# A tuned attention-plus-Fourier-plus-MLP kernel: the first part's steps taken in another written-out order, with other PSUM banks

## The chip, the cores and the metric

The kernel runs on one core of a Trainium2 chip. The metric is the device time of one execution, in microseconds (us). Engines are named as in the profile: PE is TensorE's products, PEld its weight loads, DVE is VectorE, ACT is ScalarE, POOL is GpSimd, SP is SyncE, which starts the DMAs. L766 is line 766 of the kernel. PSUM, which takes TensorE's products, is used as eight banks, numbered 0 to 7.

## The reference

Attention with positive random features, then a layer in the manner of FNet. Input are q, k and v of shape (8, 8, 576, 64), omega (128, 64), and two weight matrices, 512 x 2048 and 2048 x 512.

```
def phi(x):                                   # x: q or k times 64**-0.25
    h = x @ omega.T - sum(x * x) / 2          # 128 features
    return exp(h - max(h)) / sqrt(128)
kv  = k_p.T @ v ;  z = sum(k_p)               # for each of the 64 heads
num = q_p @ kv  ;  den = q_p @ z + 1e-6
x   = (num / den), heads side by side         # (8, 576, 512)
u   = x + real(fft(fft(x, axis=1), axis=2))
un  = layernorm(u)
out = u + relu(un @ w_ch1) @ w_ch2
```

## The kernel before, in words

The kernel has two parts, each one call of `Listing.run` (L283): part one at L1704, until about 418 us of the profiled execution, and part two at L2440. Part two does the MLP of 4096 of the 4608 rows, in a scheme that replaces eight block products by seven; its lists of the order are not touched and it is left out here.

**What part one computes.** The 64 heads are taken two at a time: 32 head pairs, four to a batch. For pair n, `attn` (L697) issues these steps:

- *Transposes of k and q*, "T": nine 128 x 128 tiles in three groups, of 4, 4 and 1 (`transposed`, the product at L636). Each group takes a bank, and ScalarE or VectorE copies it to SBUF (`evicted`, L640).
- *Scores*, "P": k and q times omega, in three groups of 4, 1 and 4 tiles (`pairs_of`, L716, the products at L731). In form Q these are products of 64 x 64 tiles, four for a tile of scores (16, 4 and 16 products), in form R of 64 x 128 tiles (8, 2 and 8); the profile counts twice as many. Each group takes two banks next to each other (a "duo"). Behind it stands the softmax: VectorE finds the maxima (L673), ScalarE takes the exponentials (L690), which also empties the banks.
- *The kv step*, "kv" (L766): 36 products in 64 x 64 tiles for one head pair, each of which the profile counts as two (x72), into a duo; `keep` (L775) copies the result out.
- *Transposes of q's features*, "E": groups of 1, 4 and 4 tiles, again at L636.
- *The nd step*, "nd" (L814 and L822): 20 products in 128 x 64 tiles, x36 in the profile, with numerator and denominator together. VectorE (or ScalarE) divides (L831 to L843), which writes x.

As soon as the four pairs of a batch are there, `mix(b)` (L855) does its Fourier transform: folds on VectorE and GpSimd (L863), two first-stage steps on TensorE (L933 and L947, here "F"), three second-stage steps (L993 and L1004, "C"), then the sum with x (`residual`, L1034) and the store of u.

Beside these run: the loads of k, q, v and the tables; the weights' conversion from the 64-bit input on ScalarE, VectorE and GpSimd (`narrow`, L548, by `weights`, L578); the MLP of the first 512 rows in the plain way, four blocks of 128 rows (`plain_of`, L1260: 16 hidden steps at L1293, "h", evicted at L1275 or L1277, and output steps at L1318, "o", which end in the addition at L1332 in `rest`, L1327); and what part two wants ready: transposed rows (`ahead`, L1633), sums of tokens (`block_norms`, L1442), of w2's parts (`w2_parts`, L1525) and of w1's parts (`weight_sums`, L1615, four sums on VectorE at L1622).

**What sets the order.** Every one of these pieces of work is a Python generator that yields a `Step` (which engines can do it, which banks and buffers it takes and gives back, which events it waits for) ahead of the instructions of that step. The head pairs are three such streams (`pairs`, L1629), of pairs 0, 3, 6, ..., of 1, 4, 7, ... and of 2, 5, 8, ...; there are thirteen streams at the start, and a stream can fork others off. `Listing.run` takes one step at a time from those that wait, and the order in which the steps are taken is the program order on each of the engines. [...]

Three written-out lists fix what it takes, for part one:

- PICKS (L68): one character a step. Its value, divided by 36, tells the engine (0 or 1, where a step can go on two), and the rest the number of the waiting stream that goes next:

```
return [divmod(DIGITS.index(c), 36) for c in text]
```

- BANKS (L91): one digit for each step that takes a bank or a duo: the bank, or the first of the two.

```
i = int(self.given[self.taken])
return i, max(t, *self.banks[i : i + n])
```

- FORMS (L101): one word for each TensorE step, read by `form()` (L421): W the whole 128 x 128 array, C 128 x 64 halves, Q 64 x 64 quarters, R 64 x 128 halves by row; two or three letters for the Fourier steps, which have several kinds of products.

The costs in the `Step`s are a planner's; where a list gives the pick they only decide nothing more than whether a step's events and buffers are there at all. A step may be taken only once everything it waits for has been taken before it; semaphores between the engines are put in from the data that the instructions read and write.

Of the kernel before, what the change touches and what calls it, by code (L numbers as in the profile page):

```python
# [41 lines left out]
class Clock(NamedTuple):  # L42
# [23 lines left out]


PICKS = (  # L68
    "1g30geg03ghid3dddehciMfegcdgej8ijgRNd8dih3gifjhbhf8hKhebgcgcijhebkl9fdcbmbN0kidhakjjdOb7f79i9baeSdja"
    "jbbScifhjgbTgfibgdijdjhjfijfabibbjdcjdiaShjhdSfdjcbfbfjjgbb9ffcgkkekhjkQecgSiki8chifjhefadfcggQgQc9d"  # L70
    "babadgcdakOb8fha8e9gfhfgg8ff1ffdPfbecffffce9e7c7fehhhbhhhhjhb8giejTijLjj7ig978ijijecdTjih8ejgfgbQgfk"
    "f88efhkkVfllWh9k9Tb8McmallmN8jkkklllkc7lmjnhfhhmoopVjcen8eaihjSbcjdekggmjbbnlohRI9linmb89eMeggWmdlhi"
    "mkeklOkfgjgURdgjbhdldkldelgmWgehkchjgifidhbbihec9fkicjbalihhbj60ijj6L96ijji7adi7edR8kjl7k6mdceeclnPe"
    "9jpfkh3Xjin95a7mekaal8bihhklmn4jgmfj7jnH8ooeeiebeko8cg9jkbifponpkpLnkkppRccSgegmmklcldX6bebdnhhWchie"
    "dSgkcmnmG7hclLaallfkjfdjnimSiiaV9ecd8kfkcT8ejjbbh6ghfd48aggghgahgcfiPghggb6gcddgg5bdhfdeiija5LjTidcc"
    "759g9gSahNce7hefigUlggck9cljafjgelagXicL8khailaRkilgiajbgeQhb7djjgihicjkahc8dbclMkhggjjcbkjjabjkkicc"
    "d7ljlaecd7ki9c5akkVbdllkaa67Klcjl9ighi6jfj77kkjIdmm9nlmlcm9loebhbno8QinZngkf#gqnpjmjkrlmj6jqknlg9llj"
    "jicjciiolii7hcQ6cafh7hgcgk59eiibibbii7Selllcl8jjml9c58ncf7dlelfFfdnm97k7l8di5lhlmm7j7lhlmen6jiLP8lgn"
    "nnnXggmmmfnoj9okfhlop8hnpllgjgIkknn9Xhhngonen9YlhjYWlhoY7hppqhr4ahlmkhffqqkqoroeqaenkdngp9ZZ955el99j"
    "ggih5kagf9n7gnd5cqcpdhfm9m9mlaXoaiJmkm8gmgnigfnnngga5akellaVacmmkVVm74cmg5mml9hgii7lllhppm9rmpptokpo"  # L80
    "qjjmqlqIo7qdlplZmoq76qqbXooknhclijlOkhgghjgf5gemijgfPiVhjUdllkhglikigLlgkGejdiPddbjkmheenganil50WWWW"
    "ma4lhfKbj5I77fJ9Mc90bebeeef4aHeadfc5aecb5fL89hObffadfgdchhcadgfhiibKS9kbgkLhgcQa9dIcbdb77gie79I8aiJU"
    "kK3hdJ9g9469Pd6baf8efe6idiajcHTT8kdbkdiien6mNpZpPpblOeOo5hePcSkLb32aHfhiSSeeaab76eiLai3ffgbfj7difmj8"
    "68dhcfil3dgl6n7nnXmWddQickli69fdiNOgaNgc9cEdI7abehijd9kkfah5Sia5aa7e9de595cad8ac24dbccb5dNbbaae6cffc"
    "hi7LO6bJbdaaddeaPb6dacgb8bfdN9b8KdfecccFgLfPRbQSi6Rc7ijhjk31O%%%%%%tjttb12f5s1J7q8aqqq89ppF5peqj4Yde"
    "enmgoXXnXgm4njQ1lj0NmLbeo33bf0dm81Un1ehAlggl60jkkQ6jjjjkjlikl9jlmiTc9ngnla08mfncgm8ogmjmccfjabib59fe"
    "hleb7j3j49djj7g7hL7h6g6QaidiIc360ff075efg5794h7a5ged7dgEhh8ffff43a094896b9b72b2baE322267360636645544"
    "43300100"
)

BANKS = (  # L91
    "3012406207460426047614204702610424206742764064210461702606425016437042604670426420340276450214620462"
    "0154240623024602432023602476105246103240736247021640524026704672047501647240264320620340260462460262"
    "4052361420652430517205647602642064605427135703462040267450231462402456406521346062023460201026026064"
    "3172260467420642301602450647201320460345627402467064246042673402646207143672167204231602465421240643"
    "7426462740516207246121046042654723450173602660512046721451706257067312"
)

FORMS = (  # L101
# [6 lines left out]
)  # L108


# [2365 lines left out]
```

## Time and profile before

| | before |
|---|---|
| median of 3 runs | 1112.19 us (1110.9 to 1112.87) |
| profiled execution | 1113.75 us |
| its span | 1112.0 us |
| granted TensorE clock in it | 1.000 |
| instructions of PE, PEld, DVE, ACT, POOL | 17759, 17759, 1685, 1644, 404 |

Part one by itself (0 to 418 us) and part two, as the view by stretches of time gives them:

```profile
0.00:418.00 418.00, 402.73 (x7850) 335.04 (x7851) 342.36 (x763) 299.47 (x1051) 185.84 (x210) 1.00 0.66 200
418.00:1112.00 694.00, 688.75 (x9911) 588.88 (x9909) 539.99 (x922) 239.18 (x593) 204.01 (x194) 1.00 0.71 221
```

In such a row stand the stretch, its length, the busy time and number of instructions of PE, PEld, DVE, ACT and POOL, the granted clock as a share of full speed, the mean busy share of the 16 DMA engines, and GB/s. In a row of the timeline stand the start in us, the length in us, the engine, the line, the operation, "out<-in" by the program's names, sizes and types, the number of instructions in the row, and in brackets the idle time before it with what ended it. In the list of waits a row names the waiting engine and line, what released it, the total in us, how often, and the longest. "issue" is idle time that nothing in the profile ended.

### The profile page before, as it was taken

The numbers are of one execution on the slowest core, as the hardware profiler recorded it, in microseconds if no ns is written. First come the engines' busy times: TensorE is split into PE (matmuls) and PEld (weight loads), VectorE is DVE, ScalarE is ACT, GpSimd is POOL, SyncE is SP. The second block draws the span as 40 slices with busy tenths as digits, with TensorE's granted clock in tenths as the row PEclk, the third lists the DMA queues.
The fourth block names the chain that finished last, engine by engine and source line by source line (L and its number), as shares of the span: only waits on it lengthen the run. The fifth ranks groups of instructions, "written<-read, shape, count | busy, mean of one in ns | idle before, by whom it ended". The sixth has DMA issues, their size and how long they took to land.

```text
span 1112.0 us, 42246 instructions
## 1 busy us (share of the span) xinstructions
PE 1091.5 (98%) x17759; PEld 923.9 (83%) x17759; DVE 882.4 (79%) x1685; ACT 538.7 (48%) x1644; POOL 389.9 (35%) x404
## 2 busy tenths in 40 slices
PE   8899999999999999999999999999999999999998
PEld 7788888878878676799998668998667999667998
DVE  6899999996776766688697777898667898668895
ACT  6988888865725554624214453223563223341221
POOL 2343444524655537733613455000365000152000
PEclk9999999999999999999999999999999999999999
DMA  7856756566665568798798768757678756556553
GB/s 230 222 177 194 242 177 202 173 191 179 222 224 211 186 183 314 228 294 299 246 300 297 215 201 254 215 158 238 203 213 259 226 156 216 174 157 220 152 160 112
DMA packets 196590, 236.80 MB, mean 213 GB/s; under 512 B 53808, under 2 KB 120624, under 8 KB 196400
## 3 DMA queue, kind: packets, MB, share of 16 engines
q1 hardware_dynamic: 195904, 233.83, 68.3%
q8 instruction: 140, 2.29, 0.9%
q14 instruction: 50, 0.41, 0.1%
q10 hardware_dynamic: 496, 0.26, 0.1%
HBM read 182.13 MB, written 56.10 MB: 214 GB/s over the span
## 4 chain that ended last, share of the span: by engine, by line
PE 92%; ACT 3%; DVE 3%; issue 1%; DMA 1%; POOL 0%; SPq 0%; DVEq 0%; ACTq 0%; POOLq 0%
PE banks L2259 30%; PE banks L1806 27%; PE banks L731 5%; PE banks L1293 5%; PE banks L1318 5%; PE banks L636 5%; PE banks L1958 4%; PE banks L766 3%; PE banks L814 2%; ACT e L690 2%; PE banks L933 2%; PE banks L993 2%; PE banks L947 1%; DVE nmx L673 1%; PE banks L822 1%
## 5 line engine op out<-in xcount | busy, mean ns | idle before, releaser
L2259 PE MATMUL banks<-wl,sums 128*64 128x128 f32 x3584 | 217.2, 273 | 0.1
L2259 PEld LDWEIGHTS banks<-wl,sums 128*64 128x64 f32 x3584 | 201.0, 137 | 2.4 <-issue 0.5
L690 ACT ACTIVATE e<-banks,nmx 128x128 f32<-128x128 f32 x576 | 161.3, 425 | 24.3 <-DVE nmx L673 23.9
L673 DVE TENSOR_REDUCE nmx<-banks 128x8 f32<-128x1024 f32 (+1 forms) x96 | 89.3, 953 | 25.6 <-PE banks L731 21.3
L2259 PE MATMUL banks<-wl,hid 128*64 128x128 f32 x1536 | 98.4, 273 | 0.5 <-DVE part L2234 0.5
L2259 PEld LDWEIGHTS banks<-wl,hid 128*64 128x64 f32 x1536 | 87.6, 137 | 1.7 <-DVE part L2234 0.7
L1806 PE MATMUL banks<-unw,wxw 128*64 128x256 f32 x704 | 85.8, 379 | 0.0
L2229 ACT ACTIVATE s<-banks 128x128 f32<-128x128 f32 x112 | 30.9, 277 | 109.7 <-PE banks L2259 109.7
L731 PE MATMUL banks<-om,kqT 64*64 64x128 f32 (+1 forms) x1988 | 81.7, 278 | 1.2 <-ACT e L690 0.8
L731 PEld LDWEIGHTS banks<-om,kqT 64*64 64x64 f32 (+1 forms) x1988 | 67.4, 143 | 12.8 <-issue 4.7
L2259 PE MATMUL banks<-wl,hx 128*64 128x128 f32 x1152 | 73.4, 273 | 0.4 <-DVE part L2234 0.4
L1806 PE MATMUL banks<-rx,wxw 128*64 128x256 f32 x576 | 71.2, 379 | 0.0
L1806 PEld LDWEIGHTS banks<-unw,wxw 128*64 128x64 f32 x704 | 50.6, 137 | 24.7
L1806 PE MATMUL banks<-ttw,wxw 128*64 128x256 f32 x576 | 70.2, 379 | 0.0
L1831 ACT ACTIVATE s<-banks 128x512 f32<-128x512 f32 x65 | 38.5, 596 | 64.2 <-PE banks L1806 59.2
L576 POOL TENSOR_TENSOR w<-w,raw 128x512 f32<-128x512 f32 x28 | 38.3, 1372 | 86.3 <-DVE raw L570 86.3
L2259 PEld LDWEIGHTS banks<-wl,hx 128*64 128x64 f32 x1152 | 65.3, 137 | 1.2 <-DVE part L2234 0.6
L1293 PE MATMUL banks<-unT,w 128*64 128x128 f32 (+1 forms) x744 | 64.5, 276 | 0.0
L2308 POOL TENSOR_TENSOR more<-more,part 128x512 f32<-128x512 f32 x2 | 2.7, 1340 | 172.6 <-ACT part L2301 172.6
L1293 PEld LDWEIGHTS banks<-unT,w 128*64 128x64 f32 (+1 forms) x744 | 58.9, 158 | 2.5 <-issue 1.2
L1318 PE MATMUL banks<-w,ht 128*128 128x512 f32 (+1 forms) x152 | 59.0, 597 | 0.0
L1806 PEld LDWEIGHTS banks<-rx,wxw 128*64 128x64 f32 x576 | 41.4, 137 | 20.2
(289 smaller groups left out, 2387.6 us busy)
## 6 DMA issues: line engine op xcount, KB each, us to landing
wl<-w2l SPq DMA_DIRECT2D x245, 256.0 KB, 3.9
wxw<-w1x SPq DMA_DIRECT2D x120, 256.0 KB, 3.2
raw<-in_moe_w_ch_dram SPq DMA_DIRECT2D x32, 512.0 KB, 4.7
kq<-in_k_dram SPq DMA_DIRECT2D x32, 288.0 KB, 4.2
kq<-in_q_dram SPq DMA_DIRECT2D x32, 288.0 KB, 4.6
vd<-in_v_dram SPq DMA_DIRECT2D x32, 288.0 KB, 5.0
ur<-us SPq DMA_DIRECT2D x30, 256.0 KB, 4.9
w2l<-sums SPq DMA_DIRECT2D x14, 512.0 KB, 3.9
```

Source lines behind the costliest of these rows:

```text
L576: eng.tensor_tensor(out=dst, in0=dst, in1=lof, op=ALU.add)
L636: nc.tensor.transpose(ps[:, (j - j0) * 128 : (j - j0 + 1) * 128], src(j), ident[:])
L673: nc.vector.tensor_reduce(nmx[:, :, 0:num], pps[:, :, 0 : MF * num].rearrange("p b (c m) -> p b c m", m=MF), axis=AX.X, op=ALU.max, negate ...
L690: nc.scalar.activation(out=e[:, c + (i if num == 1 else 0), :], in_=pps[:, i, MF * c : MF * c + MF], func=AF.Exp, bias=nmx[:, i, c : c + 1],)
L731: nc.tensor.matmul(pps[cols, c, MF * m : MF * m + MF], lhsT=kqT[rows, j, cols], rhs=om2[rows, :],)
L766: nc.tensor.matmul(kvp[cols, i, 0 : D + 1], lhsT=feature(r)[rows, cols], rhs=vds[n % NV][rows, r, :], start=(r == 0), stop=(r == R - 1),)
L1293: nc.tensor.matmul(hp[cols, 0:TP], lhsT=w1[:, dc, 128 * fc : 128 * fc + 128][:, cols], rhs=unTs[key][:, dc, :], start=(dc == 0), stop=(dc ...
L1318: nc.tensor.matmul(yp[cols, 0:DM], lhsT=hs[fc][:, 128 * i : 128 * i + 128][:, cols], rhs=w2[:, fc, :], start=(fc == 0), stop=(fc == NFC - ...
L1806: nc.tensor.matmul(ps[half, span * f : span * f + span].rearrange("f (b q) -> f b q", q=Q), lhsT=left[:, P * f : P * f + P][:, half], rhs= ...
L1831: nc.scalar.activation(out=s[:], in_=ps, func=AF.Copy)
L1958: nc.tensor.matmul(cell[half].rearrange("f t (b q) -> f t b q", q=Q), lhsT=w[:, d, col : col + 128][:, half], rhs=right[:, :, d].rearrange ...
L2259: nc.tensor.matmul(ps[half, 0:128], lhsT=left[:, f][:, half], rhs=wls[head(j), i, n][:, f], start=start and f == 0, stop=(f == 3), skip_gr ...
```

## The change

Three strings are replaced: PICKS, BANKS and FORMS of part one. Nothing else is edited. Read out with the kernel's own generators, both orders have the same 1908 steps (498 on TensorE, 463 on ScalarE, 489 on VectorE, 133 on GpSimd, 213 on SP, the others on no engine), each on the same engine and in the same form; FORMS changes only because the steps that read it come in another order. 365 of the bank digits differ. The order of SP's steps is the same.

```
 PICKS = (
-    "1g30geg03ghid3dddehciMfegcdgej8ijgRNd8dih3gifjhbhf8hKhebgcgcijhebkl9fdcbmbN0kidhakjjdOb7f79i9baeSdja"
...
+    "1g0fgf5gf04f1dhcQbe3dgdf0d6h8ShQgdibhkb6fblhfhegLjidadegigjbibgideb7fc8Rhiic8jf8fiiejablTjkjfghjfkcl"
...
 BANKS = (
-    "3012406207460426047614204702610424206742764064210461702606425016437042604670426420340276450214620462"
...
+    "0624046724650423140762062346276041602456074246020467234620642365723046204230426420340267420361420462"
...
 FORMS = (
-    "4W 2Q W R 3W 4Q 6W Q W C R 2W 2Q 3W 3Q C 3W R 2W C W 3Q 2W Q 4W 4Q C Q 7W 3Q C W WQ 3W WQ W R 2Ccz Q W 2R C 5W Q "
...
+    "4W 2Q 2W R W Q W 2Q 3W Q 3W C R Q 2W Q W Q 3W Q W Q C Q 3W R 2W C 2Q W 2Q 5W 4Q C Q 7W 3Q C W WQ 3W WQ W R 2Ccz "
...
```

What the strings mean can't be read from them. Decoded, TensorE's order around six places reads as follows (the times are those of the profile before; the number is the head pair; P8 and P32 are score groups of one and of four tiles in form Q, P16 one of four tiles in form R, by their counts of products in the profile):

| about | before | after |
|---|---|---|
| 49 us | P32(5) nd3 kv5 E5 T6 | P32(5) nd3 kv5 T6 E4 |
| 79 us | kv7 E7 E7 E7 C0 nd6 nd7 | kv7 E7 T8 T8 E6 E7 E7 C0 nd6 nd7 |
| 132 us | P kv11 P32(13) E11 h nd12 kv13 | P32(13) kv11 h E11 nd12 kv13 |
| 266 us | kv25 h kv23 E23 h E25 | kv25 P8(23) P32(23) h E25 h E24 E25 kv23 E23 E23 h E23 E25 |
| 296 us | P32(28) P8 kv26 P32(28) C C h h h | P32 P8 P32(28) kv26 h C C h h h |
| 356 us | P16(31) P16(29) kv29 kv31 E31 | P16(29) P16(31) kv31 kv29 E29 |

More of the change, by code (lines that the diff above doesn't have):

```diff
@@ L68 @@
 PICKS = (
[L69 to L88, printed above, removed]
+    "1g0fgf5gf04f1dhcQbe3dgdf0d6h8ShQgdibhkb6fblhfhegLjidadegigjbibgideb7fc8Rhiic8jf8fiiejablTjkjfghjfkcl"
@@ new lines @@
+    "heghk9lPgRhhidjiejLdkeldild9fi7fjfgkjejjjhhidcefje8gddiOge8hidlfPail7baibffbdhP7fjdjbeKebiiaTjiSaghb"
+    "dhcdca7fekPebiheeiefgahhfgfih8O1eaggegffhddhhhac977K8aiighih8hii7Sdhdj7jfjfajdiiePdgheeacifSe9efiekg"
+    "9hkkhlikUl9lVfTajRbic8iijjk8kkhkjdkMgjh9eelhoeSlciioib7n8giggon9jnffjkfjadmbaINooogaafkmeemlooUmknkl"
+    "WLagXmnmhhiemakRlgkkhkklhdfkgmhgojgWbdmJPgbfjeimljhigefbnghc6a0legfbi7e7jh67hhggbkkf7lm8kcfcelVlemmK"
+    "k6d9mnmmcklbd3gVcle8eka5k7blliellllm79jjjdnojHokolkihbaWljfmlk4jlgillaUaeimkKgnbmninebnblbbcTGkifgWf"
@@ new lines @@
+    "lfSjmagldlkklililjgbkgfeXm6hTfeghdjdTbekJ9kh8i8hf7deif4aggagghhg6eihi7jjj8Qhhfcggf79cggeedeg8ab5bf5i"
+    "gPdgeaSiSi8Pgihlk9kbieeknkelmLokkhPhfcibjagl7NdllkkeidO9i8h9jiSgiki5ch9gahRdijhfjhdi9jcjjbcbfj6hhidi"
+    "cbbfd96k88fd9ji9i978g8eMibg76kfkdigbclmk8jf9K7flhWamamccnk7jk6ki9qmoHpeZ7fg9Xnoihdnnnodlnhhpgkhnk6kg"
+    "lk8ieaajj5df6kkggdjdjjOh77idiGgcif78Riakf9lkkkk5hljjjjfeikk6mhmjecWgj7eigmfba5g78lneh6lnXbjn8nnnnclg"
+    "mmkkWbnl6lmlmfhnnkjlpihpkk9H8hhnfkhjnmmg9leVll9YljklbViojZiqgkgqrjhXmnhlkg63niawwawvadcucv+qv7axq6c6"
@@ new lines @@
+    "pu963vw8k64uqSivjvlttttoktttvophripqiruut5ouYrn&4deuhrmrjt3hqsiittluu$tvwr#weMuvefneomqqfuvusoouurrv"
+    "melejqul(poqpututslo&sssuvrwovpqSvZqqpsZtsomqnUndpsuhjmQlkjos%rj$kspmrlrqsnornqpdoilslr#rsg1pT0#ghZp"
+    "sm!k$ltgSQgpbkPbfhknhlmhbkkkiimempehgrTghiimOhnnoopgigpkkgkpgokjYkqppjURkoiQYopZZmgbjljjjfpjqljogonj"
+    "nTTjmnQYlnnhWeighXSgocmjjqoqkellQ#ppsVhpfulVjt(vntjdlkpmrVbqgn!aqchObegOWmhfUpZZbYrijrrjdpphhttMtouf"
+    "riuuosmfVslrfstYt&rptrojcvVe%ckrtgihfrqrpTfgnrqpijmdfjqpppoXkpdkmfijihfennahlcgddkgmhUjmekfopnRhmXjj"
@@ L89 @@
+    "nkhmqUYpkeeQijhnklliekhXlkllnhhhmpimmlnpN!!hkY#rpVrsbiihrphmU$ht#h%%%%%tpkttb1ssrqr1soor$sq#Ns#fqPnl"
+    "gdeNoTbhggekl0lMaOgo0a0d8Ka9dllVm0k66dkllglikj0Raiiigjhkkjdcm8O0j9l9lbflmnol8jh3nndkhg9kk8j9heh8jafe"
+    "cag3J9k9k3ba9bbifhI2Pa8fc7390dd39g50cb8a472fb5a2c8fg5afa3Chhf7g5ggg2h2g8cd9eGb7572735725077712726643"
+    "13220100"
 )
 BANKS = (
-    "3012406207460426047614204702610424206742764064210461702606425016437042604670426420340276450214620462"
-    "0154240623024602432023602476105246103240736247021640524026704672047501647240264320620340260462460262"
@@ L94 @@
-    "4052361420652430517205647602642064605427135703462040267450231462402456406521346062023460201026026064"
-    "3172260467420642301602450647201320460345627402467064246042673402646207143672167204231602465421240643"
-    "7426462740516207246121046042654723450173602660512046721451706257067312"
+    "0624046724650423140762062346276041602456074246020467234620642365723046204230426420340267420361420462"
+    "0140206405625462704670620341526250345643021624016402360462506524603210436024602167045274604602064621"
@@ L97 @@
+    "4025013426052346271462102602426402043672563075264020564250160740620465264015406260240162046706204762"
+    "0643062446026406251040624013426702406342150620456232042642304062464650175241732046025467517704260234"
+    "2650642352647346560246170426234670126374264204256071406702347046413702"
 )
 FORMS = (
[6 rows of a table removed]
[6 rows of a table added]
 )
```

12 rows, old and new, of the table FORMS are left out of this document.

## The prediction

> **What bounds the kernel now.** The page comes first: which engine is full, at what clock, and what the chain of waits is made of.
>
> ```profile
> span 1112.0 us, 42246 instructions
> PE 1091.5 (98%) x17759; PEld 923.9 (83%) x17759; DVE 882.4 (79%) x1685; ACT 538.7 (48%) x1644; POOL 389.9 (35%) x404
> ...
> PEclk9999999999999999999999999999999999999999
> ...
> q8 instruction: 140, 2.29, 0.9%
> ...
> PE 92%; ACT 3%; DVE 3%; issue 1%; DMA 1%; POOL 0%; SPq 0%; DVEq 0%; ACTq 0%; POOLq 0%
> ```
>
> TensorE is busy 98% of the span at full clock and carries 92% of the chain. An order alone can win only from the rest: 3% ScalarE, 3% VectorE, 1% "issue". Part one ends near 418 us; by stretches of 25 us it reads so (busy us of PE, PEld, DVE, ACT, POOL; clock; DMA):
>
> ```profile
> 50.00:75.00 25.00, 23.94 (x515) 20.54 (x513) 23.93 (x59) 22.53 (x85) 7.73 (x8) 1.00 0.39 128
> ...
> 100.00:125.00 25.00, 24.49 (x562) 21.79 (x561) 23.79 (x60) 20.06 (x69) 12.50 (x13) 1.00 0.81 246
> ...
> 200.00:225.00 25.00, 25.00 (x545) 21.07 (x538) 23.92 (x45) 21.82 (x81) 12.81 (x14) 1.00 0.54 164
> ...
> 250.00:275.00 25.00, 23.57 (x574) 20.80 (x574) 14.34 (x29) 14.66 (x56) 10.46 (x10) 1.00 0.58 173
> ...
> 350.00:375.00 25.00, 23.80 (x403) 18.57 (x400) 18.45 (x52) 14.89 (x54) 10.08 (x15) 1.00 0.55 189
> ```
>
> Up to about 225 us VectorE (23.8 to 23.9 of 25) and ScalarE (20 to 22.5) are nearly as full as TensorE: a microsecond saved on TensorE there is partly lost to the next wait for an eviction. After 225 us both fall to 14 to 18 of 25, and TensorE alone sets the pace: what it saves there is saved in full.
>
> Third view: TensorE's waits from 20 to 400 us (total, times, longest).
>
> ```profile
> PE banks L766 <- issue: 2.1, 3, 1.2
> PE banks L814 <- issue: 1.7, 2, 1.3
> PE banks L636 <- ACT e L690: 1.5, 4, 0.6
> PE banks L636 <- issue: 1.4, 1, 1.4
> PE banks L993 <- issue: 1.0, 1, 1.0
> PE banks L731 <- ACT e L690: 0.8, 2, 0.6
> PE banks L636 <- DVE x L843: 0.6, 2, 0.3
> PE banks L822 <- issue: 0.5, 1, 0.5
> ```
>
> The larger share, 2.1 + 1.7 + 1.4 + 1.0 + 0.5 = 6.7 us in eight idle times, is "issue": no semaphore ended it. The timeline of TensorE shows the three of over 1 us after 225 us, and the one before:
>
> ```profile
> 49.26 0.74 PE L814 MATMUL banks<-kv,qeT 128*64 128x65 f32 x18 [1.29 <-issue]
> ...
> 264.90 1.06 PE L1293 MATMUL banks<-unT,w 128*128 128x128 f32 x8
> 265.79 0.27 PE L636 MATMUL banks<-ident,e 128*128 128x128 f32 x1
> 267.50 1.91 PE L636 MATMUL banks<-ident,e 128*128 128x128 f32 x16 [1.43 <-issue]
> ...
> 296.47 0.27 PE L993 MATMUL banks<-sd_sb,y 128*64 128x128 f32 x1 [1.02 <-issue]
> ...
> 356.89 0.34 PE L766 MATMUL banks<-vd,e 64*64 64x65 f32 x6 [1.20 <-issue]
> ```
>
> They strike in the middle of a step, after a run of kv (line 766) and nd (814, 822) steps. The count of instructions between the ends of such stalls tells why:
>
> ```profile
> 49.26:79.41 30.15, 28.65 (x634) 24.92 (x634) 27.72 (x68) 27.26 (x101) 8.87 (x10) 1.00 0.48 153
> ...
> 267.50:296.46 28.97, 27.95 (x634) 26.04 (x634) 22.38 (x44) 19.04 (x71) 16.18 (x17) 1.00 0.48 138
> 296.46:356.88 60.42, 59.22 (x1018) 47.93 (x1018) 42.43 (x101) 26.44 (x92) 32.75 (x31) 1.00 0.72 245
> ```
>
> 634 products and 634 weight loads are 1268 instructions, 12 short of 5 x 256; 2 x 1018 = 2036 is 12 short of 8 x 256; a few semaphore instructions fill the difference. And q8 moved 2.29 MB in 140 packets for 2 x 17759 instructions: 254 to a packet. So TensorE's program comes in blocks of about 256, and the stall falls where a block has been issued before the next has arrived. A kv step is 72 products and 72 loads, 144 instructions in about 1.1 us; a plain first-layer step is 16 in 0.89 (264.90 to 265.79). Dense steps in one block are what empties it.
>
> [...]
>
> **The change part by part.** Read out of the new picks, every step keeps its engine and its form, and SP's 213 steps keep their order, so no DMA overtakes another on SP's queue; POOL has 25 of 133 steps out of the old order, in places up to 7 off, at 0.3 to 0.5 busy. On TensorE 138 of 498 steps leave the common order, on ScalarE 192 of 463, on VectorE 134 of 489. No instruction is added or removed. Neighbours that are both kv or nd steps fall from 16 to 13; otherwise the small products lie much as before. Lengths of blocks below are estimates, summed from the steps' own spacings in the trace.
>
> *Fetch stalls, after 225 us.* Before the 1.43 us stall stand kv of pair 25, a plain step, kv of pair 23, a transpose, a plain step. In the new order the scores of pair 23 (8 and 32 products), two plain steps and two transposes come between the two kv steps: the block of 256 held half of kv 25 (0.6 us), two plain steps (1.8), kv 23 (1.1) and two transposes (0.2), 3.7 in all; it now holds scores (0.7), the plain steps (1.8), kv 23 (1.1) and fourteen transposes at 0.11 (1.6), 5.2 in all. The 1.5 us more cover the stall: -1.4. The 1.20 us stall lies in two adjacent kv steps, pairs 29 and 31; they are still adjacent, exchanged: 0. At 296 us the kv step of pair 26 goes behind the scores of pair 28 and one plain step is put between; by the boundary the block holds as much as before: 0. A block near 335 us goes from 3.6 to 3.1 us, without a stall so far: 0, at worst +0.5. Sum -1.4, bounds -3.65 (1.43 + 1.02 + 1.20, all go) and +0.5.
>
> *Fetch stalls, before 225 us.* The 1.29 us stall stands behind scores, nd of pair 3 and kv of pair 5, unchanged in the new order: 0. Of the small ones the block at 79 us gains two steps of transposes (0.8 us, more than its idle time, 1.7 - 1.29 = 0.4), that at 39 us gains 0.4, those at 28, 132 and 211 us lose 0.9, 0.3 and 0.3. Sum about 0, bounds -1.5 and +1.
>
> *Changes of the array's shape.* The trace has a price for a step in another tile shape than its neighbours:
>
> ```profile
> 224.96 1.23 PE L766 MATMUL banks<-vd,e 64*64 64x65 f32 x72
> 226.01 0.72 PE L947 MATMUL banks<-sn_sb,fold 64*64 64x320 f32 x8
> ...
> 261.23 1.28 PE L766 MATMUL banks<-vd,e 64*64 64x65 f32 x72
> 262.44 1.16 PE L1293 MATMUL banks<-unT,w 128*128 128x128 f32 x8
> 263.52 1.28 PE L766 MATMUL banks<-vd,e 64*64 64x65 f32 x72
> ```
>
> A kv step between 64*64 neighbours takes 226.01 - 224.96 = 1.05 us, between 128*128 neighbours 262.44 - 261.23 = 1.21; a plain step between transposes 0.89, between kv steps 263.52 - 262.44 = 1.08. So one change costs about 0.17. The new order has 168 where the old has 158: +1.7 if all count. But eleven more fall in the first 100 us, and one fewer after; there the stretch 50 to 75 us has TensorE idle for 1.06 us of 25 anyway and VectorE for as little, so that part of it hides behind waits that are there: I take +0.7, bounds 0 and +1.7. [...]
>
> *Banks.* The new PSUM banks leave TensorE less room: steps that take a bank (in a few cases a tile) which an eviction has to free or fill after a step that ended less than 1 us before (counted in TensorE's own work) rise from 28 to 37, those under 0.6 us from 3 to 6. The tightest new one: nd of pair 12 takes the bank that the plain step before it fills, with one transpose of 0.11 between. The price, from that plain step as it runs now:
>
> ```profile
> 129.25 1.06 PE L1293 MATMUL banks<-unT,w 128*128 128x128 f32 x8
> ...
> 130.24 1.15 PE L814 MATMUL banks<-kv,qeT 128*64 128x65 f32 x32
> ...
> 130.47 0.28 DVE L1275 TENSOR_SCALAR ht<-banks 128x128 f32<-128x128 f32 x1
> ```
>
> The eviction ends at 130.75, 0.5 after nd began: a wait of about 0.5. (The issue idle of 0.5 in line with L822 lies in this very step, and can swallow it.) Behind a waiting nd stands all of TensorE; ScalarE and VectorE then get its product late. Two more at 0.2 each, the others nothing: +0.5, bounds 0 and +3 (nine new ones at 0.3).
>
> *The end of part one.* Three of VectorE's four w1s sums go later (by 107, 50 and 8 places). What covers them:
>
> ```profile
> 406.01 0.68 DVE L1622 TENSOR_TENSOR w1s<-w,w1s 128x512 f32<-128x512 f32 x1
> ...
> 418.15 0.69 DVE L1332 TENSOR_TENSOR ur<-ur,banks 128x512 f32<-128x512 f32 x1 [4.17 <-PE banks L1318]
> ```
>
> Three at 0.68 are 2.0 us, in an idle time of 4.17 that TensorE ends: 0. Without it, up to +2 before part two's first leaf. Part two itself begins behind TensorE's last step of part one and shifts with it.
>
> Sum: -1.4 + 0 + 0.7 + 0.5 + 0 = -0.2 us. The profiled execution took 1113.75 us, 1.75 over its span of 1112.0, and would take 1113.55. The median of the runs, 1112.19, lies 1.56 below it: 1112.0.
>
> **The rivals.** *More stalls go* (faster). What a block may take hangs on when its packet comes: full blocks elsewhere in the trace pass without a stall, so a slightly longer one may pass too, and 3 to 5 of the 6.7 us of issue idle go. For it: every stall falls behind dense steps. Against: three of the four large ones stand in the same company as before. Time: 1112.19 - 3 to - 5, about 1108.2.
>
> *New waits for evictions* (slower). Place: TensorE before nd and score steps up to 225 us, where VectorE has 1.1 us free in 25. It decides from the point where an eviction's own queue is more than 0.3 us behind: then the nine new tight banks cost 0.3 to 0.5 each, and VectorE, made late by moved weight conversions, cannot make it up: +3 to +4, about 1115.5. For it: 28 against 37. Against: the old order's tight steps (three under 0.6) cost it little.
>
> *Shape changes at full price, the 1.43 us stall moved and not gone*: +1.7 + 0.5 = +2.2, about 1114.4. For it: the rows above. Against: idle time up to 100 us.
>
> *The change does not do what it says*: the idle times called issue have another cause than full blocks, and stay. Then the first term is 0, and 0.7 + 0.5 = +1.2: 1113.4. Against: the counts of 12 short of 5 x 256 and 8 x 256. [...]
>
> **How the numbers follow.** A measurement of this kernel tells 0.2%, 2.2 us, from no change. The forecast, 0.36, reaches from 1109.3 to 1114.7: 0.08 of it faster, 0.24 same, 0.04 slower. More stalls go: 0.27, faster. New waits: 0.23, slower. Shape changes: 0.10, of it 0.06 slower and 0.04 same. Another cause: 0.04, same. Together faster 0.35, same 0.32, slower 0.33. The range takes in the first two rivals' centres: 1107.2 to 1116.0; the forecast's own is 1109.3 to 1114.7.
>
> **What would show it.** Right: TensorE's waits for issue fall from 6.7 to about 5.3, the idle time near 266 us is gone, those near 49, 296 and 356 us stay, and the stretch 225 to 275 has 1.4 us less; TensorE reaches 225 us not earlier than before. Wrong: other large issue waits gone, or new waits of TensorE on VectorE or ScalarE of over 2 us together before 225 us.

## The result, and the profile after

The changed kernel is slower: the median of 12 runs is 1116.87 us (1114.08 to 1120.14), against 1112.09 us for 12 runs of the kernel before. The ratio is 1.0041, 95% interval [1.0027, 1.0055], some 4.6 us. Forecast was 1112.0, in a range of 1107.2 to 1116.0. Both kernels' runs differ by several microseconds among themselves, so ratios are used below. The profiled execution took 1117.92 us.

The page of the changed kernel, the same parts as before:

```profile
span 1116.1 us, 42235 instructions
PE 1094.4 (98%) x17759; PEld 948.2 (85%) x17759; DVE 888.2 (80%) x1685; ACT 538.5 (48%) x1644; POOL 388.7 (35%) x404
...
PE 90%; DVE 4%; ACT 3%; issue 1%; DMA 1%; SPq 0%; DVEq 0%; ACTq 0%
```

In the chain VectorE's share goes from 3% to 4%. Where it went shows in TensorE's waits from 20 to 400 us:

```profile
PE banks L766 <- issue: 4.3, 3, 2.4
PE banks L636 <- ACT e L690: 1.1, 3, 0.6
PE banks L731 <- DVE ur L1332: 1.1, 1, 1.1
PE banks L814 <- issue: 0.8, 1, 0.8
PE banks L1004 <- issue: 0.7, 1, 0.7
PE banks L822 <- issue: 0.7, 1, 0.7
```

Two waits are new: one of 2.4 us "issue" in front of a kv step (L766), and one of 1.1 us on VectorE's L1332. The one of 1.4 us before L636 is gone. To see what each was worth, I took from each trace the time at which TensorE had done the same amount of part one's steps, each step counted by its median duration, and the difference to the kernel before. In microseconds, change of that difference by stage (stages by the time of the kernel before):

| stage | changed kernel |
|---|---|
| start to 167 us | -0.5 |
| 167 to 183 us | +4.0 |
| 183 to 258 us | +1.0 |
| 258 to 275 us | -1.7 |
| 275 to 320 us | -0.5 |
| 320 to 335 us | +1.5 |
| 335 us to the end of part one | +0.3 |
| sum | +4.1 |

The spans differ by 4.1 as well: part two shifts as a whole. So the larger part of the loss sits in two places, and the gain of 1.7 where the prediction put it. The +1.0 between 183 and 258 us was not traced to a cause; about as much stands there in sum_back and both_back below, so it is not what those runs put right.

**The first place, 177 us.** The timeline of the changed kernel, with the rows of VectorE, of GpSimd and of the kv step:

```profile
176.55 0.54 DVE L899 TENSOR_TENSOR fold<-half 128x384 f32<-128x384 f32 x1
...
177.02 0.15 DVE L909 TENSOR_TENSOR mid<-half,parted 128x6 f32<-128x6 f32 x1
177.09 0.41 DVE L1059 TENSOR_TENSOR x<-x,bmp 64x257 f32<-64x257 f32 x1
177.34 2.37 POOL L870 TENSOR_TENSOR half<-x 128x1024 f32<-128x1024 f32 x1 [1.13 <-ACT e L690]
177.43 2.56 DVE L1060 TENSOR_TENSOR x<-x,bmp 64x255 f32<-64x255 f32 x1
179.92 0.27 DVE L650 COPY kqT<-banks 128x128 f32<-128x128 f32 x1
...
180.29 0.32 PE L766 MATMUL banks<-vd,e 64*64 64x65 f32 x5 [2.44 <-issue]
```

VectorE's L1060, an addition of 64 x 255, takes 2.56 us; the same operation takes 0.41 in the kernel before (below). It starts 0.09 us after GpSimd's L870 and ends (177.43 + 2.56 = 179.99) 0.28 us after that one has ended (177.34 + 2.37 = 179.71). Both operations have two inputs in SBUF. Behind L1060 on VectorE stands L650, the eviction that frees bank 2. The kv step of pair 18 takes banks 2 and 3; it starts 0.10 us after L650 has ended (179.92 + 0.27 = 180.19). So "issue" is a wrong label here, and it is no block of 256 either. Counted in TensorE's instructions, its semaphore instructions included, the changed kernel's other five issue waits of over 0.4 us from 20 to 400 us fall at place 193 or 194 of 256; this one falls at place 94, and place 193 was passed at 174.22 and again at 181.49. The kernel before, at the same place:

```profile
175.61 0.41 DVE L1059 TENSOR_TENSOR x<-x,bmp 64x257 f32<-64x257 f32 x1
175.94 0.41 DVE L1060 TENSOR_TENSOR x<-x,bmp 64x255 f32<-64x255 f32 x1
176.27 1.01 DVE L899 TENSOR_TENSOR fold<-half 128x384 f32<-128x384 f32 x2
177.21 0.15 DVE L909 TENSOR_TENSOR mid<-half,parted 128x6 f32<-128x6 f32 x1
...
177.54 2.37 POOL L870 TENSOR_TENSOR half<-x 128x1024 f32<-128x1024 f32 x1 [1.92 <-DVE mid L909]
...
178.42 0.28 DVE L650 COPY kqT<-banks 128x128 f32<-128x128 f32 x1
```

There the sum (L1059, L1060) stands ahead of the fold step (L899, L909). The end of that fold step is what GpSimd's L870 waits for ("<-DVE mid L909"; the changed kernel's row names ScalarE, but there too L870 starts 0.17 us after L909 has ended). The change put the sum behind the very step that lets GpSimd start. L650, which reads a PSUM bank, runs beside the same GpSimd operation here in its usual 0.28.

So an addition of 0.41 us took 2.56 where it started 0.09 us into a GpSimd operation of 2.37. What holds it, the trace does not show.

The stall has a sequel. In the stretches around it (the third number from the end of a row is the granted clock; why they begin and end at these times stands in the last section):

```profile
177.02:180.44 3.42, 0.98 (x41) 0.77 (x37) 3.42 (x6) 1.20 (x5) 2.37 (x1) 1.00 0.72 241
180.44:183.85 3.41, 3.41 (x77) 3.29 (x74) 3.38 (x7) 2.18 (x8) 0.00 (x0) 0.50 0.66 207
183.85:187.27 3.42, 3.42 (x64) 2.98 (x65) 2.49 (x7) 2.05 (x9) 0.00 (x0) 1.00 0.50 155
```

After 2.4 us without a product TensorE's clock was granted at 0.50 for 3.41 us, which is at most 1.7 us lost. The wait and the clock, 2.44 + 1.7 = 4.1, make up the +4.0 of this stage. In 3 of the 12 runs the mean clock was 1.000 (1114.08 to 1115.01 us, still above the 1112.09 of before); in the eight with 0.997 or 0.998 the times are 1116.53 to 1120.14.

**The second place, 326 us**, again GpSimd, VectorE and TensorE of the changed kernel:

```profile
324.66 1.64 POOL L1060 TENSOR_TENSOR x<-x,bmp 64x255 f32<-64x255 f32 x1 [2.42 <-DVE bmp L1050]
326.26 2.50 POOL L1544 TENSOR_TENSOR big<-w,big 128x512 f32<-128x512 f32 x2
...
325.64 3.14 DVE L872 COPY half<-x 128x2 f32<-128x2 f32 x1
...
329.63 0.67 DVE L1332 TENSOR_TENSOR ur<-ur,banks 128x512 f32<-128x512 f32 x1
...
330.36 0.89 PE L731 MATMUL banks<-om,kqT 64*64 64x128 f32 x24 [1.13 <-DVE ur L1332]
```

A copy of two columns, 0.15 to 0.16 us elsewhere, is held for 3.14 us, through three GpSimd operations in a row: it ends at 328.78, the last of them at 328.76. L1332 comes after it, and frees the bank that the score step waits for. The kernel before has a hold near here too, 3.54 us where 1.22 is usual (GpSimd's two operations of L1544 run from 321.72 to 324.21), and TensorE does not wait:

```profile
321.76 3.54 DVE L870 TENSOR_TENSOR half<-x 128x1024 f32<-128x1024 f32 x1
```

There TensorE has transposes and output products to do meanwhile, and is busy from 320 to 328 us without a gap. So a hold of 3.54 us cost TensorE no wait and one of 3.14 a wait of 1.13: the difference is in what was queued behind it.

### The profile page after: what moved, and what is told of

The parts are those of the page before. It is cut to its first block, busy times and chain, and to the rows that moved or that the text cites. A ratio compares the mean times of both kernels' runs of the same rounds, so it can differ in the third digit from the quotient of the medians.

```text
span 1116.1 us, 42235 instructions
## 1 busy us (share of the span) xinstructions
PE 1094.4 (98%) x17759; PEld 948.2 (85%) x17759; DVE 888.2 (80%) x1685; ACT 538.5 (48%) x1644; POOL 388.7 (35%) x404
## 4 chain that ended last, share of the span: by engine, by line
PE 90%; DVE 4%; ACT 3%; issue 1%; DMA 1%; SPq 0%; DVEq 0%; ACTq 0%
PE banks L2259 30%; PE banks L1806 27%; PE banks L1293 5%; PE banks L636 5%; PE banks L731 5%; PE banks L1318 5%; PE banks L1958 4%; PE banks L766 3%; PE banks L814 2%; ACT e L690 2%; PE banks L993 1%; PE banks L933 1%; PE banks L947 1%; DVE nmx L673 1%; DMA kq<-in_k_dram 1%
## 5 line engine op out<-in xcount | busy, mean ns | idle before, releaser
L2259 PEld LDWEIGHTS banks<-wl,sums 128*64 128x64 f32 x3584 | 203.3, 137 | 1.8 <-issue 0.5
L1806 PEld LDWEIGHTS banks<-unw,wxw 128*64 128x64 f32 x704 | 57.9, 137 | 17.5
L1806 PEld LDWEIGHTS banks<-rx,wxw 128*64 128x64 f32 x576 | 46.9, 137 | 14.8
L1806 PEld LDWEIGHTS banks<-ttw,wxw 128*64 128x64 f32 x576 | 46.9, 137 | 14.8
```

The costliest lines, as they stand in the source:

```text
L1806: nc.tensor.matmul(ps[half, span * f : span * f + span].rearrange("f (b q) -> f b q", q=Q), lhsT=left[:, P * f : P * f + P][:, half], rhs= ...
L2259: nc.tensor.matmul(ps[half, 0:128], lhsT=left[:, f][:, half], rhs=wls[head(j), i, n][:, f], start=start and f == 0, stop=(f == 3), skip_gr ...
```

## The experiments

The theory: the change lost its time where VectorE's SBUF operations are held beside GpSimd, with an eviction behind them that TensorE waits for (2.56 and 3.14 us held, 2.44 and 1.13 waited). The expectations call it "port", the name of a mark that the kernel's planner gives to some steps of VectorE and GpSimd (L184); no run shows what holds an operation. Rivals: the new tight banks (the prediction's own rival), full blocks of instructions, or a clock that drops by itself. The diffs give the order of steps on the engine concerned, read out of the picks. A single move alters a few characters of one string, as in the first experiment:

```
-    "...HpeZ7fg9Xnoihdnnnodlnhhpgkhnk6kg"
+    "...HpjeZ7f9Yooihdnnnodlniipgkhnk6kg"
```

**One step put back** (sum_back):

```
 VectorE, changed kernel
-fold of batch 3 (L899 L909), sum of batch 2 (L1059 L1060), eviction L650
+sum of batch 2 (L1059 L1060), fold of batch 3 (L899 L909), eviction L650
```

> The changed kernel with one step of VectorE put back: the sum of batch 2's last 64 rows (L1059, L1060) again ahead of the fold step (L899, L909) whose end lets GpSimd's L870 start. Theory (port): that sum was held for 2.56 us because GpSimd's L870 runs beside it, and VectorE's eviction behind it let TensorE's kv step of pair 18 wait 2.44 us; so L1060 takes 0.42 us again, TensorE's idle time near 180 us is gone, the granted clock is 1.000 in all runs instead of 0.997 to 0.998 in most, and the time is 3.4 us below the changed kernel: about 1113.4. Rival (block): the idle time is called issue by the profile and is a full block of 256 instructions; then a step moved on VectorE changes nothing, and the time stays at 1116.9. Rival (clock alone): the clock drops by itself in this kernel; then the stall goes but 0.998 stays, and the time is about 1114.5.

Measured: 1113.02 us, ratio to the kernel before 1.0013 [1.0000, 1.0025] where the changed kernel has 1.0041. VectorE and TensorE there:

```profile
174.30 0.41 DVE L1060 TENSOR_TENSOR x<-x,bmp 64x255 f32<-64x255 f32 x1
...
176.02 1.28 PE L766 MATMUL banks<-vd,e 64*64 64x65 f32 x72 [0.30 <-ACT e L690]
```

L1060 takes 0.41 again, the kv step waits 0.30 in place of 2.44, and the stage 167 to 183 us costs 0.3 or less against the kernel before instead of 4.0. Both rivals fall: the idle time was neither a block nor a clock of its own, for in this profile the stall and the drop behind it are both gone. The expected 1.000 in all runs did not come: eight of ten have 0.999 or 1.000, two have 0.998. These two were not traced, so where their clock fell is open.

**The bank alone** (kv_bank): the kv step of pair 18 gets banks 4 and 5, and the two takers behind it are exchanged to match; three digits of BANKS (the text below says four takers).

```
-    "4025013426052346271462102602426402043672563075264020564250160740620465264015406260240162046706204762"
+    "4025013426052346271462102604246402043672563075264020564250160740620465264015406260240162046706204762"
```

> The changed kernel with one PSUM bank changed: the kv step of pair 18 takes banks 4 and 5, and the four takers behind it are exchanged likewise; no step moves on any engine. Theory (port, passed on by a bank): VectorE's L1060 is still held 2.5 us, but the kv step does not wait for the eviction behind it; TensorE's idle time near 180 us falls from 2.4 to below 0.7, the clock stays at 1.000, about 1113.7. Rival (VectorE late is TensorE late): the next step that needs VectorE, a score step or the fold's product, waits as long, and the time stays within 1 us of 1116.9. Rival (block): the idle time stays where it is, 1116.9.

Measured: 1118.18 us, ratio 1.0055 [1.0036, 1.0074], four runs.

```profile
174.01 2.57 DVE L1060 TENSOR_TENSOR x<-x,bmp 64x255 f32<-64x255 f32 x1
...
176.83 1.35 PE L933 MATMUL banks<-cs_sb,fold 128*128 128x160 f32 x8 [0.72 <-DVE kqT L650]
...
177.94 2.17 ACT L690 ACTIVATE e<-banks,nmx 128x128 f32<-128x128 f32 x8 [3.16 <-DVE nmx L673]
...
183.20 1.74 PE L814 MATMUL banks<-kv,qeT 128*64 128x65 f32 x32 [1.88 <-ACT e L690]
```

The kv step waits 0.32 and not 2.44, but the fold's product waits 0.72 for L650, ScalarE waits 3.16 for VectorE's late maxima, the nd step waits 1.88 for ScalarE's exponentials, and the clock fell to 0.50 here too. My expectation was wrong. The rival is right in kind, though it named a score step or the fold's product and a time within 1 us of 1116.9 (it is 1.3 above, with four runs): with VectorE 2.1 us late, other steps of TensorE met the delay under this bank too.

**The other step put back** (rest_back):

```
 VectorE, changed kernel
-fold of batch 6: L870, L872, L876; output of plain rows L1332
+fold of batch 6: L870; output of plain rows L1332; fold: L872, L876
```

> The changed kernel with another step of VectorE put back: the addition of the plain rows' output (L1332) again ahead of the fold's small copy and sums (L872, L876). Theory (port): near 326 us L872 is held 3.14 us instead of 0.16 by three operations of GpSimd in a row, and L1332 behind it frees the bank that the score step waits for; ahead of it L1332 is not held, and the wait of L731 on L1332, 1.1 us, is gone: 1.3 us below the changed kernel, about 1115.6. Rival: the score step waits for the softmax behind the held L872 just as long: no change, 1116.9.

Measured: 1115.81 us, ratio 1.0030 [1.0017, 1.0042], 1.2 us below the changed kernel by the ratios. The two intervals overlap, so the time alone does not show the gain; the trace shows the wait gone. L872 now takes 0.59, L1332 is at 326.02 and the score step does not wait:

```profile
326.02 0.69 DVE L1332 TENSOR_TENSOR ur<-ur,banks 128x512 f32<-128x512 f32 x1 [1.88 <-PE banks L1318]
326.62 0.59 DVE L872 COPY half<-x 128x2 f32<-128x2 f32 x1
```

In the stage 320 to 335 us the +1.5 are gone (-0.1).

**Both put back** (both_back).

> The changed kernel with both steps of VectorE put back. Theory (port): these two places are all that the change lost beside what it won, so the time is 4.7 us below the changed kernel, 1112.2, and at most 0.2% from the kernel before; TensorE's issue waits are those of the changed kernel without the one of 2.4 us. Rival (banks): the nine new tight banks cost several small waits as well; then the sum falls short, and the time stays above 1114.

Measured: 1111.73 us, ratio 0.9995 [0.9981, 1.0008]: two steps of VectorE undo the loss, and what is left of the change cannot be told from the kernel before. One and the same block stall differs between executions by over a microsecond: near 48 us, where both have the same steps, this profile has 2.1 and the changed kernel's 0.8,

```profile
PE banks L814 <- issue: 2.1, 1, 2.1
```

and the clock stayed at 1.00 behind it.

**The loss made in the old order** (sum_late): the kernel before, with its sum moved behind the fold step; its banks kept.

```
 VectorE, kernel before
-sum of batch 2 (L1059 L1060), fold of batch 3 (L899 L909)
+fold of batch 3 (L899 L909), sum of batch 2 (L1059 L1060)
```

> The kernel before with one step of VectorE moved as the changed kernel has it: the sum of batch 2's last 64 rows behind the fold step whose end lets GpSimd's L870 start; banks and all other steps as before. Theory (port): L1060 is held for over 2 us there too, VectorE's maxima and eviction behind it come late, and TensorE waits 1 to 2.4 us near 180 us, for a score or nd step, since the kv step's banks are not behind VectorE here; the granted clock falls below 1.000 in some runs; 1113.5 to 1116. Rival (the new banks are needed too): the hold is there, and TensorE doesn't wait, 1112.3.

Measured: 1115.45 us, ratio 1.0026 [1.0014, 1.0039].

```profile
175.83 2.58 DVE L1060 TENSOR_TENSOR x<-x,bmp 64x255 f32<-64x255 f32 x1
...
179.79 1.35 PE L933 MATMUL banks<-cs_sb,fold 128*128 128x160 f32 x8 [1.57 <-DVE kqT L650]
```

One exchange of two VectorE steps brings the hold (2.58) and a wait of 1.57 into the old order. So neither the new banks nor the rest of the new order is needed for the loss. The stage 167 to 183 us costs +1.8 and not 4.0: the wait is shorter, and the profiled clock stayed at 1.000. By the ratio the loss is 2.9 us; the traced run, 1114.64, is 0.8 below the median, and the rest was not traced.

**GpSimd's operation in two halves** (pool_split), in the changed kernel; one line more, so L1060 is L1061 in its profile.

```
-eng.tensor_tensor(out=h[:, 0:NL], in0=x[:, 0:NL], in1=x[:, NL : 2 * NL], op=op)
+for c0, c1 in ((0, 1), (1, NL)) if (b, n) == (3, 1) else ((0, NL),):
+    eng.tensor_tensor(out=h[:, c0:c1], in0=x[:, c0:c1], in1=x[:, NL + c0 : NL + c1], op=op)
```

> The changed kernel, with GpSimd's first fold operation of batch 3 (L870, 2.37 us) issued as two of half the columns each; order, banks and results as in the changed kernel. Theory (port, held for one instruction): VectorE's L1060 waits only for the first half, takes 1.4 us instead of 2.56, TensorE's idle time near 180 us falls from 2.4 to about 1.2, and the clock stays at 1.000: 1114.5. Rival (held until GpSimd pauses): L1060 takes 2.5 us or more as before, and the time stays at 1116.9.

Measured: 1115.42 us, ratio 1.0020 [1.0009, 1.0031].

```profile
175.31 1.48 DVE L1061 TENSOR_TENSOR x<-x,bmp 64x255 f32<-64x255 f32 x1
...
175.22 2.71 POOL L871 TENSOR_TENSOR half<-x 128x512 f32<-128x512 f32 x2 [1.13 <-ACT e L690]
...
176.72 0.27 DVE L650 COPY kqT<-banks 128x128 f32<-128x128 f32 x1
...
177.09 1.28 PE L766 MATMUL banks<-vd,e 64*64 64x65 f32 x72 [1.36 <-ACT e L690]
```

The hold is 1.48, the kv step waits 1.36 (it starts 0.10 us after L650, as in the changed kernel), and nine of ten runs have a clock of 0.999 or 1.000. No order and no bank changed here, only the length of GpSimd's instruction: the first half takes 1.29, and L1061 ends 0.28 us after it, as L1060 ended 0.28 us after the whole one in the changed kernel. The expected 1114.5 was counted from 1112.09 for the kernel before; on that scale the ratio gives about 1114.3.

**Kv steps set apart in the kernel before**, which tests the prediction's own theory, the blocks: pair 23's kv step and its first transpose moved behind one plain step and three transpose steps (kv23_later); pair 31's behind one plain step, with other banks for the plain steps there (kv31_later); both (kv_apart).

```
 TensorE, kernel before
-kv25 h kv23 E23 h E25 E25 E25 E23 E23
+kv25 h h E25 E25 E25 kv23 E23 E23 E23
-kv29 kv31 E31 E29 h h
+kv29 h kv31 E31 E29 h
```

> The kernel before with the kv step of pair 23 (and its first transpose) moved behind the plain step and the three transpose steps of pair 25, so that 1.9 us of other work stand between the two kv steps near 265 us. Theory (block): the idle time of 1.4 us in line with L636 near 267 us falls to below 0.4, and none of over 0.5 us comes up where the three nd steps stand behind; 1.2 us below the kernel before: 1111.1. Rival (the stall moves): one of about 1.4 us at the next boundary, near 273 us: 1112.3.

> The kernel before with the kv step of pair 31 (and its first transpose) behind one plain step, so that the kv steps of pairs 29 and 31 near 354 us no longer touch; the plain steps take other banks. Theory (block): the idle time of 1.2 us in L766 near 356 us falls to 0.3 to 0.5, for 0.9 us of other work come into the block: 1111.4. Rival: the plain step waits for the softmax that empties its bank, as long as the stall was: 1112.3.

> Both moves in the kernel before, kv of pair 23 and kv of pair 31. Theory (block): the two add up, 1110.2, faster than both kernels by 0.2%. Rival: the first moves the boundary of all later blocks in time only, not in count, so nothing else is expected; if the stalls near 296 us grow instead, 1111.5.

Measured: ratios 1.0002 [0.9990, 1.0013], 1.0009 [0.9994, 1.0024], 1.0006 [0.9994, 1.0018]. No gain. The traces of kv23_later and kv31_later say why:

```profile
263.92 1.16 PE L1293 MATMUL banks<-unT,w 128*128 128x128 f32 x8 [0.42 <-ACT e L690]
```

```profile
354.92 1.16 PE L1293 MATMUL banks<-unT,w 128*128 128x128 f32 x8 [1.59 <-ACT e L690]
```

The block stalls did go, each where its step was moved: the 1.43 us near 267 us in kv23_later, which has no issue wait from 258 to 272 us, and the 1.20 near 356 us in kv31_later, which has none from 350 to 358. But the plain step that now comes earlier waits for an exponential to free its bank, 0.4 and 1.6 us. In its stage kv23_later gains 0.6; kv31_later loses 0.8. The block theory of the stall holds: in the trace of before, the seven issue waits of over 0.4 us from 20 to 400 us all end at place 193 of 256, 1.2 to 1.6 us after a packet of 16384 bytes on q8 has landed. Its price does not. The likely reason is that ScalarE had caught up while TensorE stood still; no run here tests that by itself.

**Two steps put back and kv31, kv29 apart** (three), on the changed kernel:

```
 TensorE, changed kernel
-kv31 kv29 E29 h
+kv31 h kv29 E29
```

> The changed kernel with both steps of VectorE put back, and beside it one plain step between the kv steps of pairs 31 and 29, which touch. Theory (block): the idle time of 1.2 to 1.6 us in L766 near 356 us goes; the plain step waits about 0.7 us for VectorE's copy of pair 31's result; 0.6 us below the kernel with two steps put back (1111.7): 1111.1, 1.2 us faster than the kernel before. Rival: the plain step's wait is as long as the stall, 1111.7, or longer, as with the move of pair 31 in the kernel before.

Measured: 1112.49 us, ratio 0.9998 [0.9985, 1.0011]. The stall is gone, the plain step waits 0.56 for VectorE's copy:

```profile
354.08 1.16 PE L1293 MATMUL banks<-unT,w 128*128 128x128 f32 x8 [0.56 <-DVE kv L780]
```

None of the versions is shown to be faster than the kernel before.

## Why the prediction was wrong

- *The step that failed* is in the first lines of "The change part by part": "POOL has 25 of 133 steps out of the old order, in places up to 7 off, at 0.3 to 0.5 busy", with nothing charged for it, and VectorE's 134 moved steps not laid beside GpSimd's. Neither was a matter of how busy GpSimd is. Two exchanges on VectorE brought an SBUF operation beside a running GpSimd one. It took 2.1 and 3.0 us longer than usual (2.56 for 0.41, 3.14 for 0.16), and behind it stood a step that frees a bank. The exchanges cost 4.0 and 1.5 us by stage, and putting them back takes the ratio from 1.0041 to 0.9995. The trace of before showed the price, in the view of one line's instructions (shortest, median and longest in ns):

```profile
L870 DVE TENSOR_TENSOR half<-x x11: 1164/1224/3540, 51.7 to 380.3; 128x1024 f32<-128x1024 f32 x11
```

```profile
L1060 DVE TENSOR_TENSOR x<-x,bmp x13: 409/418/1520, 108.2 to 407.0; 128x255 f32<-128x255 f32 x11, 64x255 f32<-64x255 f32 x2
```

  One operation with two durations: the prediction did not ask why.
- *A second term stood nowhere in the sum: the clock.* It was taken as 1.00 throughout; after the stall it was 0.50 for 3.41 us, 1.7 of the 4.0 us at the first place.
- *"After 225 us both fall to 14 to 18 of 25, and TensorE alone sets the pace"* was read off two stretches. VectorE was busy 23.16 of 25 us from 225 to 250 and 20.56 from 275 to 300, and the second place, at 326 us, lies where VectorE has room on average: one hold ahead of the wrong step is enough for +1.5.
- *The rival "new waits for evictions"* named 1115.5 and the right kind of end, a wait of TensorE behind a late VectorE, and the text's own mark for it ("new waits of TensorE on VectorE or ScalarE of over 2 us together before 225 us") is what came. Its cause was wrong: not nine tight banks at 0.3 to 0.5; that its time comes near 1116.87 is chance. The tightest, nd of pair 12, shows no wait in front of it in the changed kernel, and other banks for the kv step (kv_bank) did not help. The +0.5 for banks was not seen; both_back, whose interval reaches 0.9 us above the kernel before, cannot exclude it.

```profile
129.18 0.27 PE L636 MATMUL banks<-ident,e 128*128 128x128 f32 x1
129.38 1.15 PE L814 MATMUL banks<-kv,qeT 128*64 128x65 f32 x32
```

- *Shape changes, +0.7:* not seen, and not excluded. Up to 167 us, where eleven more of them lie, the changed kernel is 0.5 us ahead; but executions of the same steps differ there by more than the term: pair 18's kv step starts at 176.02 in sum_back's profile and at 178.29 in both_back's.
- *The 1.43 us stall goes, -1.4:* right, -1.7 in its stage, and again in sum_back and both_back (-1.7).
- *The stalls near 49, 296 and 356 us stay:* right in kind (0.8, 0.7 and one of over a microsecond are there). Without the mislabelled 2.4 the issue waits come to 4.1, where 5.3 were expected. That each term is worth its trace value was too simple, since both_back has 2.1 at 48 us with the same steps around it.
- *The end of part one, 0:* right; the lag of 4.1 there is the difference of the spans.
- *"Another cause than full blocks"* was priced at 0.04 for all issue waits. The largest issue wait after the change was indeed another thing: VectorE's eviction, mislabelled.

## What to carry to other kernels

When an order is changed, lay VectorE's SBUF operations beside GpSimd's, operation by operation, and ask what each one's end releases: here an addition moved behind the step that lets GpSimd start was held until GpSimd's instruction of 2.37 us had ended, 2.56 us in place of 0.41, and so was everything queued behind it. An operation that shows two durations in the trace of before, here 418 and 1520 ns or 1224 and 3540, hints at the price in advance. The length of a stall of the busiest engine is not what its removal pays: the 1.43 us stall near 267 us was worth 1.7 in the changed order and 0.6 in kv23_later, where the next step had to wait for ScalarE.

## What was not expected of the hardware

- The granted clock fell to half after some stalls of TensorE and not after others, and the length of the stall does not sort them: it fell after 1.73 us near 39 us in kv23_later, and stayed at 1.00 after 2.09 us near 48 us in both_back. A grid in time does. By the traces' clock records, the full clock lasted 170.67 us up to the drop in the changed kernel and in rest_back, 174.08 in kv_bank and 30.72 in kv23_later, which are 50, 51 and 9 times 3.413 us; each of these four drops lasted 3.413 us. Taken on this grid, kv23_later (two rows), both_back (two) and kv31_later read:

```profile
36.68:40.09 3.41, 1.52 (x74) 1.20 (x70) 3.05 (x5) 1.99 (x8) 2.11 (x2) 1.00 1.09 194
40.09:43.50 3.41, 3.41 (x63) 2.75 (x58) 1.45 (x3) 1.65 (x7) 1.11 (x1) 0.50 0.79 232
```

```profile
43.90:47.31 3.41, 2.55 (x114) 2.24 (x105) 3.34 (x6) 3.15 (x13) 1.36 (x2) 1.00 0.98 310
47.31:50.73 3.42, 2.20 (x98) 2.06 (x98) 1.11 (x4) 2.17 (x8) 1.16 (x1) 1.00 0.40 121
```

```profile
264.33:267.75 3.42, 1.74 (x17) 1.61 (x16) 0.79 (x3) 0.91 (x6) 1.05 (x1) 1.00 0.84 209
```

  The stall of both_back is divided between two stretches, which are idle 0.9 and 1.2 us, and the clock stays. In all twelve traces, from the first full clock to the last 10 us, four stretches of the grid are idle for 1.89 us or more (kv23_later 1.89, kv_bank 1.92, the changed kernel and rest_back 2.44), and half the clock follows each; none of the others is idle for more than 1.68 (the row of kv31_later), and full clock follows all of them. So in these runs the line lies between 1.68 and 1.89 us of idle time in one stretch; what sets it no run shows. This would also fit the changed kernel's runs without a drop, but those were not traced.
- A copy of two columns on VectorE (L872) was held through three GpSimd operations, 3.14 us, and did not get in between them, while in pool_split the addition L1061 ended 0.28 us after the first of two halves. What makes the difference was not tried.
